# Six small transfers of each segment: issued by SyncE instead of GpSimd

## The chip, the core and the metric

The kernel runs on one core of one Trainium2 chip. The core has TensorE (matrix products, PE in the profile; its weight loads are PEld), VectorE (DVE), ScalarE (ACT), GpSimd (POOL) and SyncE (SP), which computes nothing and here issues most of the transfers. Sixteen DMA engines move the data. The metric is the device time of one execution in microseconds (us); the time of a kernel is the median of several runs.

## The reference

Two independent parts stand side by side in the output, 1024 columns each. Part A is a long convolution over 2048 rows, done with Fourier transforms; it is over before the loop that this document is about. Part B is an attention with a memory that is handed from segment to segment:

```python
for s in range(n_seg):                       # 2048 / 32 = 64 segments
    h = concatenate([mem, x[:, 32*s:32*s+32]], axis=1)      # 8 + 32 rows of 1024
    q, k, v = (einsum('btd,dhe->bhte', h, W) for W in (Wq, Wk, Wv))   # 32 heads of 128
    p = softmax(where(mask, einsum('bhqe,bhke->bhqk', q, k) * scale, -1e9))
    o = einsum('bhqk,bhke->bhqe', p, v)
    o = einsum('bhte,hed->btd', o, Wo)
    mem = o[:, :8]                           # the next segment's memory
    outs.append(o[:, 8:])                    # 32 rows of the result
```

The first 8 rows of a segment's output are needed before the next segment can start, so the 64 segments run one after the other. Every segment uses all four weights, 8 MB each in bf16.

## The kernel before

**The order.** The program is unrolled and its order is the order of the text: each engine works off its own instructions in the order in which they stand. A transfer is an instruction in the stream of the engine that issues it, and that engine goes on as soon as it has handed the transfer over. An instruction that must wait stops what stands behind it on the same engine, transfers too. The profile calls the issuing streams SPq, ACTq and POOLq. Transfers that SyncE issues run in DMA queue q1, those of ScalarE in q10, those of GpSimd in q0.

**The rows.** In the loop (L910) a segment's part on TensorE has 32 rows: 8 of the memory and the first 24 of the segment. The last 8 rows of every segment do not feed the memory. Their q, k and v are made for all segments ahead of the loop and lie in HBM, in `QKBd` and `VBd`. A segment loads its share of them: `qkb` (`load_b`, L793, 128 KB) and `VB` (`load_vb`, L803, 64 KB). Their attention outputs are gathered in `OL` and stored to `OLd` (L860, 64 KB), and their output projection is done for all segments behind the loop (L977 on).

**The weights.** Most of the weights stay in SBUF. Of each segment's weights, 17 pieces of 512 KB (`streamed`, chosen by `STREAM`, L40) come from HBM every time, and two more are parked in PSUM and copied from there (`PARKED`, L41; `unpark`, L716). They go through a ring of `RING = 5` buffers (L39, tile `wring`). `done(key)` (L725) is called behind the last matmul that reads a streamed piece, and `place()` (L708) then issues the load of the piece five places on into the freed buffer, at L713, on SyncE. So a load is issued when TensorE has finished with a piece, and at most five pieces are loaded or being loaded at a time.

**A segment** has four groups `g` of eight heads. `qk_part` makes q and k of a group, `v_part` its v; `scores`, `softmax` and `pv` of a group lie between the products of later groups, and `wo` adds the output projection into the accumulator `Y`. The end of a segment reads: `wo` of group 0, `v_part` of group 3, the load of the next rows (`load_h`, L662, ScalarE), `load_b` for the next segment, `wo` of group 1, `wo` of group 2, `pv` of group 3 with the copy of the last rows' outputs into `OL` (L858, GpSimd) and their store, `wo` of group 3, the copy of `Y` into `Y_sb` (L964, ScalarE), the turn of the memory rows into the next `hT` (`fill_mem`, L965), four stores of `Y_sb` to the result (L970, 12 KB each: 24 rows of 512 bytes), and `load_vb` for the next segment.

**Names for the loads.** Later sections number the 17 weight loads of a segment in the order of their issue. Those around the end are W14 (issued when the second piece of `wo` of group 1 is finished), W15 and W16 (pieces 0 and 3 of `wo` of group 2), W17 (piece 2 of `wo` of group 3), and, in the next segment, W1 (behind `qk_part` piece 5 of group 0), W2 and W3 (behind the first two pieces of `v_part` of group 0). The four stores of `Y_sb` are o1 to o4. With `qkb` the SyncE stream at the end of a segment before the change is: W12, W13, `qkb`, W14, W15, W16, W17, W1, W2, W3. GpSimd's is: copy into `OL`, store of `OL`, o1, o2, o3, o4, load of `VB`.

**Who needs them.** `VB` is read by `pv`, first for group 0 when group 2 is under way. `OL` is written again by the copy of group 0 of the next segment. `Y_sb` shares its one buffer (tag `PT`) with the transposed probabilities of L838, so the softmax of the next segment's group 0 must wait until o1 to o4 have read it. Nobody waits for what the stores wrote to the result.

Of the kernel before, what the change touches and what calls it, by code (L numbers as in the profile page):

```python
# [21 lines left out]
def fused_kernel(ctx: ExitStack, tc, q, k, v, shift_k, ssm_k, ssm_D, outa, x, mem0, Wq, Wk, Wv, Wo, outb, n_seg):  # L22
# [11 lines left out]
    nc = tc.nc  # L34
# [17 lines left out]
    OLd = dram.tile([n_seg, 128, 256], BF, name="OLd")  # L52
    VBd = dram.tile([n_seg, 4, 4, 8, 256], BF, name="VBd")
# [662 lines left out]
    def unpark():  # L716
        while to_copy:
            key, t = to_copy.pop(0)
            nc.scalar.copy(t[:, 0, :], park[key][0][:])  # L719
            nc.vector.tensor_copy(t[:, 1, :], park[key][1][:])  # L720
# [14 lines left out]
    VB = act.tile([128, 256], BF, name="VB")  # L735
    OL = act.tile([128, 32, 8], BF, name="OL")
# [5 lines left out]
    def qk_part(u, kcs):  # L742
        if kcs[0] == 0:
            u.qk = ps_qk.tile([128, 512], F32, tag="qk", name="qkacc")
        for kc in kcs:
            w = pair(("qk", u.g, kc))
            for t in range(2):
                for c2 in range(2):
                    p0 = 32 * (2 * t + c2)
                    nc.tensor.matmul(u.qk[p0:p0 + 32, :], lhsT=hT[:, kc, :], rhs=w[t][:, c2 * 512:(c2 + 1) * 512],  # L750
                                     start=(kc == 0), stop=(kc == 7), tile_position=(0, p0))
            done(("qk", u.g, kc))

    def qk_out(u):
        u.qks = act.tile([128, 512], BF, tag="qks", name="qks")
        nc.scalar.copy(u.qks[:], u.qk[:])  # L756
# [39 lines left out]
    def new_u(g):  # L796
        u = G()
        u.g = g
        u.qkb = qkb[:, g, :]
        return u  # L800

    def load_vb(s):
        nc.gpsimd.dma_start(VB[:], VBd[s].rearrange("c g r x -> (c g r) x"))  # L803

    def scores(u):
        S = ps_ts.tile([128, 4, 40], F32, tag="ts", name="S")
        qb = u.qkb.rearrange("e (h t r) -> e h t r", h=8, t=2)
        for c in range(4):
            nc.tensor.matmul(S[32 * c:32 * c + 32].rearrange("p a k -> p (a k)"), lhsT=ident[:, 32 * c:32 * c + 32],
                             rhs=mask[:].unsqueeze(2).to_broadcast([128, 2, 2, 40]), start=True, stop=False,  # L810
                             tile_position=(0, 32 * c))
        for i in range(2):
            for c in range(4):
                hh = 2 * c + i
                nc.tensor.matmul(S[32 * c:32 * c + 32, i, :], lhsT=u.QT[:, hh, :], rhs=u.KT[:, hh, :],
                                 start=False, stop=False, tile_position=(0, 32 * c))
        for i in range(2):
            for c in range(4):
                hh = 2 * c + i
                nc.tensor.matmul(S[32 * c:32 * c + 8, 2 + i, :], lhsT=qb[:, hh, 0, :], rhs=u.KT[:, hh, :],  # L820
                                 start=False, stop=(i == 1), tile_position=(0, 32 * c))
        mx = act.tile([128, 4], F32, tag="mx", name="mx")
        nc.vector.tensor_reduce(out=mx[:], in_=S[:], op=ALU.max, axis=AX.X)  # L823
        nc.vector.tensor_tensor(out=S[:], in0=S[:], in1=mx[:].unsqueeze(2).to_broadcast([128, 4, 40]), op=ALU.subtract)
        return S

    def softmax(u, S):
        P = act.tile([128, 4, 64], BF, tag="QTP", name="P")
        k0 = 32 + 8 * u.g
        nc.vector.memset(P[:, :, 32:64], 0.0)  # L830
        nc.scalar.activation(P[:, :, 0:32], S[:, :, 0:32], ACT.Exp, scale=scale)
        nc.scalar.activation(P[:, :, k0:k0 + 8], S[:, :, 32:40], ACT.Exp, scale=scale)  # L832
        sm = act.tile([128, 4], F32, tag="sm", name="sm")
        nc.vector.tensor_reduce(out=sm[:], in_=P[:], op=ALU.add, axis=AX.X)  # L834
        nc.vector.reciprocal(sm[:], sm[:])
        nc.vector.tensor_tensor(out=P[:], in0=P[:], in1=sm[:].unsqueeze(2).to_broadcast([128, 4, 64]), op=ALU.mult)
        u.PT = act.tile([128, 4, 2, 32], BF, tag="PT", name="PT")
        nc.vector.transpose(out=u.PT[:].rearrange("p a k q -> p (a k q)"), in_=P[:].rearrange("p a k -> p (a k)"))  # L838

    def pv(u, s, cs, banks="aaaa"):  # L840
        if cs[0] == 0:
            u.OT = act2.tile([128, 8, 40], BF, tag="OT", name="OT")
        PTv = u.PT[:].rearrange("p (a i) k q -> p i k a q", a=2)
        for c in cs:
            pool, tag = {"a": (ps_acc, "acc"), "q": (ps_qk, "qk"), "t": (ps_ts, "ts")}[banks[c]]
            ot = pool.tile([128, 512], F32, tag=tag, name="otacc")
            r = slice(32 * c, 32 * c + 32)
            for i in range(2):
                o = ot[:, 64 * i:64 * i + 64]
                nc.tensor.matmul(o, lhsT=u.v[r, i * 128:(i + 1) * 128], rhs=PTv[r, i, 0], start=True, stop=False,  # L850
                                 tile_position=(32 * c, 0))
                nc.tensor.matmul(o, lhsT=VB[r, i * 128:(i + 1) * 128], rhs=PTv[r, i, 1], start=False, stop=True,  # L852
                                 tile_position=(32 * c, 0))
            ov = ot[:, 0:128].rearrange("e (i q) -> e i q", i=2)
            nc.scalar.copy(u.OT[:, 2 * c:2 * c + 2, :], ov[:, :, 0:40])  # L855
        if cs[-1] == 3:
            to = OL[:] if s + 1 < n_seg else OLs[:, s]
            nc.gpsimd.tensor_copy(to[:, 8 * u.g:8 * u.g + 8, :], u.OT[:, :, 32:40])  # L858
            if u.g == 3 and s + 1 < n_seg:
                nc.gpsimd.dma_start(OLd[s], OL[:].rearrange("e h r -> e (h r)"))  # L860

    def wo(u, Y, hhs=range(8)):
        for hh in hhs:
# [46 lines left out]
    for s in range(n_seg):  # L910
        us = []
        for g in range(4):
            if g == 2 and s + 1 == n_seg:
                spare = [key for key in resident if key[0] != "o" and key[1] < 2 and key not in early]
                for key, at in zip([key for key in streamed if key[0] == "o"], spare):
                    nc.sync.dma_start(res[at][:], Wst[key][:])
                    res[key] = res[at]
            u = new_u(g)
            us.append(u)
            qk_part(u, range(0, 4))  # L920
            unpark()
            if g >= 1:
                S = scores(us[g - 1])
            if g >= 2:
                pv(us[g - 2], s, (0, 1))
            if g >= 1:
                softmax(us[g - 1], S)
            qk_part(u, range(4, 6))
            if g >= 2:
                pv(us[g - 2], s, (2, 3))  # L930
            qk_part(u, range(6, 8))
            qk_out(u)
            if g < 3:
                v_part(u, range(0, 8))
                tr_a(u)
                v_out(u)
            unpark()
            if g == 3 and s + 1 == n_seg:
                for s0, s1 in ((0, 32), (32, s)):
                    nc.sync.dma_start(OLs[:, s0:s1].rearrange("e s h r -> e s (h r)"),  # L940
                                      OLd[s0:s1].rearrange("s e x -> e s x"))
        Y = ps_acc.tile([128, 512], F32, tag="acc", name="yacc")
        wo(us[0], Y)
        tr_a(us[3])
        v_part(us[3], range(0, 8), Y)
        v_out(us[3])
        if s + 1 < n_seg:
            H = load_h(s + 1)
        S = scores(us[3])
        if s + 1 < n_seg:  # L950
            qkb = load_b(s + 1)
        softmax(us[3], S)
        pv(us[2], s, (0, 1), "aqaq")
        wo(us[1], Y, range(0, 4))
        pv(us[2], s, (2, 3), "aqaq")
        wo(us[1], Y, range(4, 8))
        wo(us[2], Y)
        pv(us[3], s, (0, 1, 2, 3), "aqta")
        wo(us[3], Y)
        if s + 1 < n_seg:  # L960
            hT = new_hT()
            h_rows(H, hT, 8)
        Y_sb = act.tile([128, 256], BF, tag="PT", name="Y_sb")
        nc.scalar.copy(Y_sb[:], Y[:, 256:512])  # L964
        if s + 1 < n_seg:  # L965
            fill_mem(hT, Y_sb)
            idle = ps_acc.tile([128, 512], F32, tag="acc", name="idle")
            keep_warm(idle, 2)
        for dq in range(4):
            nc.gpsimd.dma_start(outb[32 * s:32 * s + 24, dq * 256:(dq + 1) * 256], Y_sb[32 * dq + 8:32 * dq + 32, :])  # L970
        if s + 1 < n_seg:
            load_vb(s + 1)

# [87 lines left out]
```

## Time and profile before

| | |
|---|---|
| median of 3 runs | 2194.64 us (2191.91 to 2197.0) |
| the profiled execution's own time | 2189.17 us |
| its span, first to last instruction | 2187.2 us |
| mean granted TensorE clock | 0.956 |
| first and last copy into `Y_sb` (64 segments) | 488.2 and 2125.9 us |
| busy: TensorE, VectorE, ScalarE, GpSimd | 1783.4, 1090.5, 835.3, 405.9 us |
| issue of a weight load on SyncE (L713), median | 320 ns, 1083 of them |
| issue on GpSimd: one store of `Y_sb`, store of `OL`, load of `VB`, median | 508, 547, 563 ns |
| the same from issue to landing, median | 4.8, 5.4, 4.8 us |

The page gives for each engine its busy time and for the 16 DMA engines their mean busy share. From the copies into `Y_sb` the period of the loop follows: the 63rd was at 2094.1 us, so 62 periods took 1605.9 us, 25.9 us each. The rest of the execution lies in part A, ahead of the loop, and in the last rows' projection behind it. A line of the chain of waits says which work or transfer ended last at each point; a line of the waits says who waited, for whom, how long in total, how often, and the longest.

### The profile page before, as it was taken

What the parts mean: (1) busy time and instruction counts of PE and PEld (TensorE: products, weight loads), DVE (VectorE), ACT (ScalarE), POOL (GpSimd) and SP (SyncE); (2) the same over time, 40 slices, a digit from 0 to 9 for tenths busy, and PEclk for the clock granted to TensorE, in tenths of its full rate; (3) what the DMA queues carried; (4) which work ended last, traced back from release to release, by engine and by line L of the source; (5) the groups of instructions that cost most, each with busy time, mean ns of one, the idle gap of its engine ahead of it and who ended that gap; (6) DMA issues with size and microseconds to landing.
All of it is one profiled execution on the core that took longest, in us unless ns stands there. A gap on an engine that the chain in (4) does not pass through costs nothing.

```text
span 2187.2 us, 87959 instructions
## 1 busy us (share of the span) xinstructions
PE 1783.4 (82%) x37808; PEld 1048.2 (48%) x37808; DVE 1090.5 (50%) x3235; ACT 835.3 (38%) x2538; POOL 405.9 (19%) x841
## 2 busy tenths in 40 slices
PE   5777778758888888888888888888888888888889
PEld 2332223325555555554555555545555555555558
DVE  6885652224454555544455455444554545444540
ACT  5445551123333333333444333333333333334320
POOL 4013562101111111111111111111111111111110
PEclk8989899879999999999999999999999999999999
DMA  7798969889999999999999999999999999999990
GB/s 256 266 312 273 314 233 330 267 288 353 347 356 343 373 374 365 368 364 347 370 372 371 370 354 370 362 358 355 368 366 354 363 356 357 371 362 367 359 335 21
DMA packets 275653, 732.15 MB, mean 335 GB/s; under 512 B 65680, under 2 KB 85024, under 8 KB 275262
## 3 DMA queue, kind: packets, MB, share of 16 engines
q1 hardware_dynamic: 214414, 683.05, 84.7%
q0 software_dynamic: 18368, 28.88, 4.2%
q10 hardware_dynamic: 42480, 14.62, 2.7%
q8 instruction: 295, 4.83, 0.9%
q14 instruction: 96, 0.78, 0.1%
HBM read 676.14 MB, written 59.18 MB: 336 GB/s over the span
## 4 chain that ended last, share of the span: by engine, by line
PE 47%; DMA 36%; issue 6%; DVE 4%; ACT 4%; POOL 1%; SPq 0%; ACTq 0%; DVEq 0%; POOLq 0%
DMA wring<-Wstv 17%; PE qkacc L750 13%; PE yacc L867 9%; DMA wring<-Wstqk 7%; PE vacc L765 4%; PE otacc L850 3%; PE yacc L765 3%; PE tp L779 3%; PE pl L984 3%; DMA QKBd<-stq 2%; DMA H<-in_B_x_dram 2%; PE ps_k L177 2%; PE otacc L852 1%; DMA wring<-Wsto 1%; PE ps_q L177 1%
## 5 line engine op out<-in xcount | busy, mean ns | idle before, releaser
L750 PE MATMUL qkacc<-Wqk,hT 128*32 128x512 bf16 x4096 | 351.8, 384 | 3.6 <-issue 3.5
L855 ACT CAST OT<-otacc 128x80 bf16<-128x80 f32 x1024 | 183.8, 235 | 387.4 <-PE otacc L852 381.3
L858 POOL COPY OL<-OT 128x64 bf16<-128x64 bf16 x252 | 63.9, 253 | 1362.3 <-ACT OT L855 1362.3
L765 PEld LDWEIGHTS <-hT 128*32 128x32 bf16 x8192 | 213.8, 97 | 168.7 <-issue 101.9
L750 PEld LDWEIGHTS <-hT 128*32 128x32 bf16 x8192 | 178.3, 96 | 209.9 <-issue 66.7
L867 PE MATMUL yacc<-Wo,OT 128*32 128x256 bf16 x5632 | 253.3, 282 | 26.6 <-issue 21.2
L867 PEld LDWEIGHTS <-OT 128*32 128x32 bf16 x8192 | 213.1, 99 | 90.4 <-issue 58.4
L750 PE MATMUL qkacc<-wring,hT 128*32 128x512 bf16 x2048 | 207.1, 390 | 22.7 <-DMA wring<-Wstqk 20.3
L850 PE MATMUL otacc<-PT,vsb 32*128 32x64 bf16 x2048 | 147.7, 193 | 55.5 <-ACT OT L855 48.7
L765 PE MATMUL vacc<-wring,hT 128*32 128x256 bf16 x2560 | 118.0, 277 | 74.7 <-DMA wring<-Wstv 73.5
L788 DVE COPY QT<-tp 128x256 bf16<-128x256 bf16 x256 | 74.7, 292 | 204.7 <-PE tp L779 198.7
L719 ACT COPY wring<-park 128x1024 bf16<-128x1024 bf16 x128 | 129.9, 1015 | 116.2 <-PE qkacc L750 110.0
L750 PE MATMUL qkacc<-Wearly,hT 128*32 128x512 bf16 x2048 | 167.7, 403 | 7.7 <-DVE hT L893 3.4
L756 ACT CAST qks<-qkacc 128x512 bf16<-128x512 f32 x256 | 150.3, 587 | 47.6 <-PE qkacc L750 44.5
L823 DVE TENSOR_REDUCE mx<-S 128x4 f32<-128x160 f32 x256 | 83.1, 325 | 163.8 <-PE S L820 160.7
L765 PE MATMUL vacc<-Wv,hT 128*32 128x256 bf16 x3584 | 158.4, 274 | 0.7 <-issue 0.7
L834 DVE TENSOR_REDUCE sm<-P 128x4 f32<-128x256 bf16 x256 | 107.5, 420 | 100.6 <-ACT P L832 100.6
L852 PE MATMUL otacc<-PT,VB 32*128 32x64 bf16 x2048 | 144.2, 189 | 11.2 <-issue 10.5
L867 PE MATMUL yacc<-wring,OT 128*32 128x256 bf16 x2520 | 137.1, 281 | 16.4 <-issue 15.4
L885 DVE COPY hT<-x_tp 128x192 bf16<-128x192 bf16 (+1 forms) x64 | 23.0, 359 | 233.8 <-PE x_tp L884 233.8
L970 POOL DMA_DIRECT2D out_dram<-Y_sb x256 | 129.1, 511 | 39.6 <-ACT Y_sb L964 36.3
L850 PEld LDWEIGHTS <-vsb 32*128 32x128 bf16 x2048 | 84.3, 92 | 103.8 <-issue 94.1
(220 smaller groups left out, 2931.9 us busy)
## 6 DMA issues: line engine op xcount, KB each, us to landing
wring<-Wstqk SPq DMA_DIRECT2D x448, 512.0 KB, 6.4
wring<-Wstv SPq DMA_DIRECT2D x320, 512.0 KB, 6.0
wring<-Wsto SPq DMA_DIRECT2D x315, 512.0 KB, 6.0
SK<-s_sb SPq DMA_DIRECT2D x8, 1024.0 KB, 6.5
SU<-s_sb SPq DMA_DIRECT2D x8, 1024.0 KB, 7.8
QKBd<-stq ACTq DMA_DIRECT2D x4, 2048.0 KB, 16.3
Kg<-SK SPq DMA_DIRECT2D x16, 512.0 KB, 6.1
Ug<-SU SPq DMA_DIRECT2D x16, 512.0 KB, 7.2
```

The costliest lines, as they stand in the source:

```text
L719: nc.scalar.copy(t[:, 0, :], park[key][0][:])
L750: nc.tensor.matmul(u.qk[p0:p0 + 32, :], lhsT=hT[:, kc, :], rhs=w[t][:, c2 * 512:(c2 + 1) * 512], start=(kc == 0), stop=(kc == 7), tile_pos ...
L756: nc.scalar.copy(u.qks[:], u.qk[:])
L765: nc.tensor.matmul(u.vacc[32 * c:32 * c + 32, 0:256], lhsT=hT[:, kc, :], rhs=w[kc % 2][:, c * 256:(c + 1) * 256], start=(kc == 0 and Y is ...
L788: nc.vector.tensor_copy(u.QT[:].rearrange("e (c j) r -> e c j r", c=2), tv[:, 0])
L823: nc.vector.tensor_reduce(out=mx[:], in_=S[:], op=ALU.max, axis=AX.X)
L834: nc.vector.tensor_reduce(out=sm[:], in_=P[:], op=ALU.add, axis=AX.X)
L850: nc.tensor.matmul(o, lhsT=u.v[r, i * 128:(i + 1) * 128], rhs=PTv[r, i, 0], start=True, stop=False, tile_position=(32 * c, 0))
L852: nc.tensor.matmul(o, lhsT=VB[r, i * 128:(i + 1) * 128], rhs=PTv[r, i, 1], start=False, stop=True, tile_position=(32 * c, 0))
L855: nc.scalar.copy(u.OT[:, 2 * c:2 * c + 2, :], ov[:, :, 0:40])
L867: nc.tensor.matmul(Y[32 * dq:32 * dq + 32, 256:512], lhsT=u.OT[:, hh, 0:32], rhs=w[hh % 2][:, dq * 256:(dq + 1) * 256], start=(u.g == 0 an ...
L970: nc.gpsimd.dma_start(outb[32 * s:32 * s + 24, dq * 256:(dq + 1) * 256], Y_sb[32 * dq + 8:32 * dq + 32, :])
```

## The change

Three calls change their engine, nothing else:

```diff
     def load_vb(s):
-        nc.gpsimd.dma_start(VB[:], VBd[s].rearrange("c g r x -> (c g r) x"))
+        nc.sync.dma_start(VB[:], VBd[s].rearrange("c g r x -> (c g r) x"))
...
             if u.g == 3 and s + 1 < n_seg:
-                nc.gpsimd.dma_start(OLd[s], OL[:].rearrange("e h r -> e (h r)"))
+                nc.sync.dma_start(OLd[s], OL[:].rearrange("e h r -> e (h r)"))
...
         for dq in range(4):
-            nc.gpsimd.dma_start(outb[32 * s:32 * s + 24, dq * 256:(dq + 1) * 256], Y_sb[32 * dq + 8:32 * dq + 32, :])
+            nc.sync.dma_start(outb[32 * s:32 * s + 24, dq * 256:(dq + 1) * 256], Y_sb[32 * dq + 8:32 * dq + 32, :])
```

In the loop GpSimd keeps its copies into `OL` (L858) and issues no transfer any more. The stream of SyncE at the end of a segment becomes: W12, W13, `qkb`, W14, W15, W16, store of `OL`, W17, o1, o2, o3, o4, load of `VB`, W1, W2, W3. The first `load_vb(0)`, ahead of the loop, moves too. The transfers have the same sources, targets and sizes as before.

## The prediction

> **What bounds the kernel now.** I read the page first (DMA row, chain of waits), then the DMA queues over the loop, then the waits, and then one segment's end in time order: SyncE, GpSimd, chain, and the windows of one microsecond.
>
> ```profile
> DMA  7798969889999999999999999999999999999990
> PE 47%; DMA 36%; issue 6%; DVE 4%; ACT 4%; POOL 1%; SPq 0%; ACTq 0%; DVEq 0%; POOLq 0%
> ```
>
> The DMA engines are busy from the first quarter to the end, and the chain has TensorE and DMA but almost no GpSimd. The queues between 500 and 2100 us, and two waits of TensorE there:
>
> ```profile
> q1 hardware_dynamic: 160270, 559.20, 93.7%
> q0 software_dynamic: 11890, 11.19, 2.3%
> ```
>
> ```profile
> PE vacc L765 <- DMA wring<-Wstv: 60.4, 100, 2.3
> PE qkacc L750 <- DMA wring<-Wstqk: 19.6, 37, 1.4
> ```
>
> With q10, q8 and q14 (0.9, 1.1, 0.1%) the shares add up to 98.1%: the DMA engines' time is the bound, and TensorE waits for weights. What GpSimd issues is 2.3% of it and stays; only its queue changes. So the question is what the move does to the idle 2% and to the time of a packet. One segment's end (SyncE, then GpSimd, then the chain; columns are start, us, what):
>
> ```profile
> 1008.39 0.97 SPq L713 DMA_DIRECT2D wring<-Wstv  x2
> 1010.67 0.32 SPq L713 DMA_DIRECT2D wring<-Wstqk  x1
> 1013.91 0.32 SPq L713 DMA_DIRECT2D wring<-Wstv  x1
> ```
>
> ```profile
> 1010.18 0.24 POOL L858 COPY OL<-OT 128x64 bf16<-128x64 bf16 x1 [1.93 <-ACT OT L855]
> 1010.71 0.55 POOL L860 DMA_DIRECT2D OLd<-OL  x1 [0.29 <-POOL OL L858]
> 1011.55 2.02 POOL L970 DMA_DIRECT2D out_dram<-Y_sb  x4 [0.30 <-ACT Y_sb L964]
> 1013.56 0.56 POOL L803 DMA_DIRECT2D VB<-VBd  x1
> ```
>
> ```profile
> 1012.39 1.51 PE qkacc L750 x24
> 1013.91 5.75 DMA wring<-Wstv
> 1019.70 0.84 PE vacc L765 x24
> ```
>
> W15 and W16 go out from 1008.39 (the second at 1009.04), W17 at 1010.67, and W1 at 1013.91, as soon as TensorE has freed its buffer. W1 is on the chain: its landing at 1019.66 is what TensorE waits for. Where DMA engines idle (the last two columns are DMA share and GB/s):
>
> ```profile
> 1012.00:1013.00 1.00, 0.78 (x14) 0.33 (x16) 0.34 (x2) 0.00 (x0) 1.00 (x3) 1.00 0.90 348
> 1016.00:1017.00 1.00, 1.00 (x40) 0.50 (x32) 0.82 (x3) 0.70 (x1) 0.00 (x0) 1.00 0.80 303
> 1018.00:1019.00 1.00, 0.39 (x5) 0.12 (x6) 0.60 (x3) 0.88 (x3) 0.00 (x0) 1.00 0.84 295
> 1022.00:1023.00 1.00, 1.00 (x32) 0.47 (x32) 0.77 (x3) 0.47 (x3) 0.00 (x0) 1.00 1.02 397
> ```
>
> Early in a segment the share falls to 0.8 to 0.9, later it is full. Over 60 segments, with Y the start of o1, the packets give 0.86 to 0.96 from Y+2.5 to Y+5 and about 1.0 from Y+10 to Y+18. The segment's end is already the thin place of the weights' queue.
>
> **A rule of the transfers that the change meets.** In the issue records each transfer of SyncE or ScalarE takes the next of eight semaphores (100, 102 to 107, 109) in turn, 187 each. Over all pairs whose landing the trace has, none is issued less than 0.02 us after the landing of its semaphore's last user, and many just then. One such wait is visible where no data is shared, a weight load behind ScalarE's store of q and k, eight places earlier:
>
> ```profile
> SPq L678 <- DMA QKBd<-stq: 12.6, 1, 12.6
> ```
>
> So a transfer waits for the landing of the eighth before it. With 19 per segment (17 weights, `qkb`, H) and a ring of five, this never bites in the loop. The change makes it 25, and in the stream W14, W15, W16, store of `OL`, W17, o1 to o4, `VB`, W1, W2, W3 it binds: o4 waits for W14, `VB` for W15, **W1 for W16**, W2 for the store of `OL`, W3 for W17. GpSimd's transfers had eight semaphores of their own (111 to 118).
>
> **The parts.**
>
> *GpSimd loses six issues*, 4 x 0.508 + 0.547 + 0.563 = 3.1 us per segment. It waits 1287.5 us of the loop for `OT`, and nobody waits for it but these transfers: nothing gained.
>
> *SyncE issues six more.* Nearest rows: 0.377 us (`qkb`), 0.421 (final stores, L992). 6 x 0.4 = 2.4 us, beside 18 x 0.32 = 5.8 now, in 25.9: hidden, since o1 to o3 are out by Y+1.2 and W1's buffer is freed at Y+2.0 (median). The store of `OL` stands ahead of W17; the copy ends at 1010.42, so W17 moves from 1010.67 to about 1010.9. Cover: W17 lands 5.7 us after issue, while the quickest load of L713 takes 3.3. Without it, 0.25 x 62 = 16 us.
>
> *o1 to o4 and `VB` in the weights' queue.* They run behind W17 and land near Y+6; from GpSimd, with 4.8 us from issue, they landed at Y+6.3 and Y+6.8. The next writer of their buffer (transpose L838) starts at 1019.46, Y+7.9, and `pv` reads `VB` at Y+10.4. Nothing.
>
> *The packets.* Per segment q0 now has 32 of 4096 bytes at 187 ns, 48 of 1024 at 49 and 111 small ones at 9.1: 9.35 us, 0.58 per DMA engine. On q1 I expect pieces of 512 bytes as on q10 (27.3 ns for H's): 352 x 27.3 + 80 x 9.1 = 10.34 us, 0.65 per engine. That is +0.06 us, or 4 us over the loop. The four stores have 12 packets of two rows each; if the same 12 engines take them every time, those get 24 x 27.3 + 6 x 9.1 = 0.71 us, +0.13, or 8 us. I take 5.
> By the Trainium skill ("DMA: Bandwidth & Descriptors", section "Why a DMA increments its semaphore by 16 and not by 1") a transfer uses the largest number of engines up to 16 that divides its slowest dimension, the lowest-numbered ones on this path. For 24 rows that is always the same 12; by it the term is 8. No row here numbers the engines.
>
> *The wait of W1.* In 60 segments the medians are: W14 lands at Y+0.78, W15 at Y+2.17, W16 at Y+3.67, W17 at Y+5.22; W1 is issued at Y+2.03, W3 at Y+3.61. If W1 must wait for W16 (and `VB` for W15 ahead of it), it goes out 1.53 us later on average; W3 waits for W17, 1.6 later. From issue to first packet takes 1.57 us at the quick end (first landing of a DMA engine less the 1.26 us that 8 packets take there). So the packets of W1 can start at about Y+5.3. An engine is done with W17 between Y+3.2 and Y+5.2, then has 0.65 us of small packets, and then nothing. From each engine's landings I get a mean idle of 0.98 us per segment, against 0.42 worked out in the same way for now: +0.55. Lower bound 0: slow engines set the landing of W1, and they aren't out of work (W17 at Y+5.2, small packets until Y+5.9). Upper bound: all 1.53 us on the path, 62 x 1.53 = 95 us. Some comes back: the fast engines are less far ahead afterwards, and of the 0.05 x 4.5 = 0.2 us that is idle now from Y+5 to Y+9.5 most should fill. I take 0.35, as the DMA time of a segment is the bound: 62 x 0.35 = 22 us.
>
> **Sum:** 0 + 0 + 0 + 5 + 22 = +27 us. Against the profiled execution's own 2189.17 us (span 2187.2 plus 2.0 around it) that is 2216; the median of the runs shown is 5.5 us above it, so I forecast 2194.64 + 27 = **2222 us**, slower by 1.2%. Its own range: 0.1 to 0.55 us of idling and 4 to 8 us of packets, 2205 to 2237; with W17's 16 us, 2253.
>
> **Rivals.**
>
> *The wait is hidden.* For it: W1 lands 5.2 us after issue at the median, and 3.3 is possible; the slack of 1.9 us exceeds the delay of 1.53. Against: the 3.3 are of an empty queue. Then only the packets cost, at times less: 2191 to 2203, likeliest 2198.
> The Trainium skill ("DMA: Bandwidth & Descriptors", section "Issuing engines are not separate DMA queues") speaks for this result: whoever issues, the same 16 DMA engines move the data, and only issue time on the sequencer changes. The shares that add up to 98.1% agree; the eight semaphores are what that section leaves out.
>
> *Faster.* Packets of 4096 bytes on q0 can be long: the loads of `VB` average 205 ns against a usual 159, up to 2008. In the segment shown W1's last engine comes 3.3 us after W17's, where the median is 1.8. The longest q0 packet of a segment has a median of 0.39 us; if it always lies on the engine that lands last, and short pieces remove it, 62 x (0.39 - 0.16) = 14 us go: 2181. It decides where the delay of W1 stays within its slack. Against it: q1 has 30 packets over 0.5 us per segment of its own.
>
> *The whole delay shows.* Were W1's landing governed by its issue, all 95 us would come: 2290. The chain has W1 on it; against it, the 5.75 us there are mostly queueing.
>
> *The semaphores aren't shared in this way:* that is the first rival again.
>
> **How the numbers follow.** Chances: forecast 0.60, hidden 0.18, faster 0.15, whole delay 0.07. What can be told from no change here is 0.2%, about 4.4 us: 2190.2 to 2199. Slower: 0.60 + 0.07 + the hidden case's upper part, 0.05 = 0.72; same: 0.12 of the hidden case; faster: 0.15 and 0.01 of it. The range from 2182 to 2252 leaves out the whole delay, half of the faster case and a little of the forecast's top.
>
> **What would show it.** q0 gone from the loop, and q1 with some 430 more packets per segment, at about 27 ns. W1 issued just behind W16's landing, near Y+3.7 instead of Y+2.0, with SyncE waiting at L803 or L970 for weights. The DMA share between Y+3 and Y+5.5 lower than 0.86, the loop's mean share down from 98.1% to about 97%, the period up from 25.9 to 26.3 us. GpSimd's waits mean nothing. Wrong: if W1 goes out at Y+2 as before, the semaphore rule is not as read; if it goes out late and the period stays, the slow engines alone set the pace; if L838 or `pv` wait for o4 or `VB`, I have missed a wait.

## The result, and the profile after

| | before | changed |
|---|---|---|
| median | 2193.27 us (4 runs, 2183.92 to 2197.0) | 2218.55 us (4 runs, 2213.92 to 2224.78) |
| ratio, 95% interval | | 1.0123 (1.009 to 1.0155) |
| ratio in a second set, on another chip | 2190.49 us | 2217.22 us, 1.0107 (1.0076 to 1.0138) |
| profiled execution's own time, span | 2189.17, 2187.2 us | 2214.47, 2212.6 us |
| first and last copy into `Y_sb` | 488.2, 2125.9 us | 482.8, 2150.7 us |

The changed kernel is slower by 25 us, 1.2%. In the two profiled executions the loop itself, from the first copy into `Y_sb` to the last, is 30.2 us longer (1637.7 and 1667.9). The part ahead of it is 5.4 us shorter in the changed execution; in the other profiled executions of this study the first copy lies anywhere from 482.8 to 489.0.

The chain of waits of the changed kernel, by engine and by line:

```profile
PE 44%; DMA 42%; issue 5%; DVE 4%; ACT 4%; POOL 1%; SPq 1%; ACTq 0%; DVEq 0%; POOLq 0%
DMA wring<-Wstv 24%; PE qkacc L750 11%; PE yacc L867 9%; DMA wring<-Wstqk 7%; PE vacc L765 3%; PE yacc L765 3%; DMA wring<-Wsto 3%; PE otacc L850 3%; PE pl L984 3%; PE tp L779 2%; DMA QKBd<-stq 2%; PE ps_k L177 2%; PE ps_q L177 1%; PE ps_v L174 1%; PE otacc L852 1%
```

The second of these lines, for the kernel before:

```profile
DMA wring<-Wstv 17%; PE qkacc L750 13%; PE yacc L867 9%; DMA wring<-Wstqk 7%; PE vacc L765 4%; PE otacc L850 3%; PE yacc L765 3%; PE tp L779 3%; PE pl L984 3%; DMA QKBd<-stq 2%; DMA H<-in_B_x_dram 2%; PE ps_k L177 2%; PE otacc L852 1%; DMA wring<-Wsto 1%; PE ps_q L177 1%
```

The queues of the changed kernel between 500 and 2100 us (packets, MB, share of the 16 DMA engines):

```profile
q1 hardware_dynamic: 183630, 559.73, 93.5%
q8 instruction: 262, 4.29, 1.1%
q10 hardware_dynamic: 8784, 4.00, 0.9%
q14 instruction: 78, 0.64, 0.1%
```

DMA has gone from 36% to 42% of the chain, nearly all of it in loads of v weights (17% to 24%); W1 and W4, among the first loads of a segment, are such loads. GpSimd's queue q0 is gone. Yet the shares now add up to 95.6% where they were 98.1%: the DMA engines, which bound the loop, have less to do per unit of time. The waits in the same stretch (engine, line, what it waited for, us in total, times, longest):

```profile
PE vacc L765 <- DMA wring<-Wstv: 76.4, 125, 2.5
PE qkacc L750 <- DMA wring<-Wstqk: 39.2, 55, 1.9
```

```profile
SPq L860 <- POOL OL L858: 72.3, 61, 3.1
SPq L803 <- DMA wring<-Wstv: 29.2, 34, 2.3
SPq L970 <- DMA wring<-Wstqk: 6.4, 12, 1.0
```

TensorE waits longer for weights (60.4 and 19.6 us before). SyncE waits at L803 and L970 for the landing of weights: the load of `VB` and the stores of `Y_sb` share no data with a weight. One segment's end on SyncE, whose copy into `Y_sb` starts at 1009.80:

```profile
1007.30 0.97 SPq L713 DMA_DIRECT2D wring<-Wstv  x2
1009.42 0.39 SPq L860 DMA_DIRECT2D OLd<-OL  x1
1009.90 0.38 SPq L713 DMA_DIRECT2D wring<-Wstqk  x1
1010.38 1.64 SPq L970 DMA_DIRECT2D out_dram<-Y_sb  x4
1012.88 0.35 SPq L803 DMA_DIRECT2D VB<-VBd  x1
1014.20 0.35 SPq L713 DMA_DIRECT2D wring<-Wstv  x1
1014.65 1.36 SPq L713 DMA_DIRECT2D wring<-Wstqk  x2
```

After o4 the stream stands until 1012.88, and after `VB` until 1014.20, when W1 goes out 4.4 us behind the copy. The trace shows which semaphore each instruction sets and waits for: W16 set 104, and the wait of W1 that ended at 1014.2 was for 104, which W1 then uses itself. In the same way o4 waited for 102 (W14) and `VB` for 103 (W15). What that leaves for the DMA engines (last two columns: share and GB/s):

```profile
1013.00:1014.00 1.00, 1.00 (x36) 0.74 (x25) 0.24 (x2) 0.93 (x2) 0.00 (x0) 1.00 0.97 374
1014.00:1015.00 1.00, 0.95 (x24) 0.46 (x19) 0.05 (x1) 0.49 (x3) 0.00 (x0) 1.00 0.59 191
1015.00:1016.00 1.00, 1.00 (x29) 0.46 (x25) 1.00 (x3) 0.92 (x2) 0.00 (x0) 1.00 0.81 209
1017.00:1018.00 1.00, 0.65 (x28) 0.45 (x23) 0.59 (x3) 0.84 (x3) 0.00 (x0) 1.00 0.45 143
```

From 1014 on the engines run out of weights; in the window that starts there small packets take half of the busy time, and 191 GB/s are moved. Over 60 segments the packets fill 0.68 of the engines' time from 3 to 5.5 us behind the start of o1, where they filled 0.93 before. Over the same 60 segments, in us behind the start of the copy into `Y_sb`:

| mean | W16 lands | W17 lands | W1 issued | W1 lands | W3 issued | W3 lands |
|---|---|---|---|---|---|---|
| before | 4.34 | 5.87 | 2.93 | 7.93 | 4.38 | 10.98 |
| changed | 4.13 | 5.74 | 4.28 | 8.19 | 5.90 | 11.85 |

W1 goes out just behind the landing of W16, W3 behind that of W17. What reaches TensorE is a fifth of W1's delay (0.26 of 1.35 us), but more than half of W3's (0.87 of 1.52).

### The profile page after: what moved, and what is told of

Read it like the earlier page. It is cut to its first block, busy times and chain, and to the rows that moved or that the text cites. A ratio compares the mean times of both kernels' runs of the same rounds, so it can differ in the third digit from the quotient of the medians.

```text
span 2212.6 us, 87953 instructions
## 1 busy us (share of the span) xinstructions
PE 1781.1 (80%) x37808; PEld 1050.7 (47%) x37808; DVE 1089.4 (49%) x3235; ACT 836.2 (38%) x2538; POOL 205.7 (9%) x458
## 4 chain that ended last, share of the span: by engine, by line
PE 44%; DMA 42%; issue 5%; DVE 4%; ACT 4%; POOL 1%; SPq 1%; ACTq 0%; DVEq 0%; POOLq 0%
DMA wring<-Wstv 24%; PE qkacc L750 11%; PE yacc L867 9%; DMA wring<-Wstqk 7%; PE vacc L765 3%; PE yacc L765 3%; DMA wring<-Wsto 3%; PE otacc L850 3%; PE pl L984 3%; PE tp L779 2%; DMA QKBd<-stq 2%; PE ps_k L177 2%; PE ps_q L177 1%; PE ps_v L174 1%; PE otacc L852 1%
## 5 line engine op out<-in xcount | busy, mean ns | idle before, releaser
L858 POOL COPY OL<-OT 128x64 bf16<-128x64 bf16 x252 | 62.5, 248 | 1647.2 <-ACT OT L855 1647.2
L765 PE MATMUL vacc<-wring,hT 128*32 128x256 bf16 x2560 | 116.8, 275 | 96.5 <-DMA wring<-Wstv 94.9
L719 ACT COPY wring<-park 128x1024 bf16<-128x1024 bf16 x128 | 129.9, 1015 | 116.3 <-PE qkacc L750 99.3
L750 PE MATMUL qkacc<-Wearly,hT 128*32 128x512 bf16 x2048 | 163.0, 395 | 7.7 <-DVE hT L893 3.8
L774 ACT CAST vsb<-vacc 128x256 bf16<-128x256 f32 x192 | 71.5, 373 | 162.6 <-PE vacc L765 162.3
```

The source lines that it names most:

```text
L765: nc.tensor.matmul(u.vacc[32 * c:32 * c + 32, 0:256], lhsT=hT[:, kc, :], rhs=w[kc % 2][:, c * 256:(c + 1) * 256], start=(kc == 0 and Y is ...
L774: nc.scalar.copy(u.v[:], u.vacc[:, 0:256])
```

## The experiments

Three theories stood against each other. **The count:** transfers of SyncE and ScalarE take eight semaphores in turn, so each waits for the landing of the eighth before it, and the six more push W1 to W3 up against W16 and W17. **The queue:** small packets among the weights, some of them on 12 of the 16 engines only, cost DMA time. **The order:** SyncE's stream stands at the waits for `OL` and `Y_sb`, and weight loads stand behind it. Each kernel was timed beside the kernel before on the same chip.

### One half of the change, then the other

e1_stores moves o1 to o4 only:

```diff
-            nc.gpsimd.dma_start(outb[32 * s:32 * s + 24, dq * 256:(dq + 1) * 256], Y_sb[32 * dq + 8:32 * dq + 32, :])
+            nc.sync.dma_start(outb[32 * s:32 * s + 24, dq * 256:(dq + 1) * 256], Y_sb[32 * dq + 8:32 * dq + 32, :])
```

> The four stores of Y_sb are issued by SyncE, the store of OL and the load of VB stay on GpSimd. Theory of the count (the eighth transfer back must have landed): 23 transfers per segment; the eighth before W1 is W14, before W2 W15, before W3 W16. In the kernel before these land before or just as W1, W2 and W3 are issued (W16 at 4.34 us after the copy into Y_sb, W3 at 4.38), so the time is that of the kernel before, 0 to +6 us, and W1 goes out near 2.9 us after the copy. Theory of the queue (small packets among the weights, twelve engines carrying the stores): these stores are the part that is uneven, so a third to two thirds of the 25 us, +8 to +16. Theory of the order (SyncE's stream stands at the wait for Y_sb): up to half, +12.

Measured: 2186.89 against 2192.15 us, ratio 0.9978 (0.9954 to 1.0003).

e2_ol_vb moves the other two only:

```diff
-        nc.gpsimd.dma_start(VB[:], VBd[s].rearrange("c g r x -> (c g r) x"))
+        nc.sync.dma_start(VB[:], VBd[s].rearrange("c g r x -> (c g r) x"))
...
-                nc.gpsimd.dma_start(OLd[s], OL[:].rearrange("e h r -> e (h r)"))
+                nc.sync.dma_start(OLd[s], OL[:].rearrange("e h r -> e (h r)"))
```

> The store of OL and the load of VB are issued by SyncE, the four stores of Y_sb stay on GpSimd. Theory of the count: 21 transfers per segment, the eighth before W1 was issued ahead of W14 and has long landed: 0 to +4 us. Theory of the queue: two thirds of the 432 small packets are here, +8 to +16 us. Theory of the order: the store of OL, which waits for GpSimd's copy, is the only moved transfer with a weight load (W17) right behind it; if that wait cost the time, most of it is here, +10 to +25 us.

Measured: 2183.75 against 2192.15 us, ratio 0.998 (0.9951 to 1.0009).

Each half alone costs nothing; if anything it gives 0.2%, which the intervals don't settle. Together they cost 1.2%. A price per transfer, per packet or per wait in the stream would add up; a limit that is reached only by both does not. W1 goes out at 2.95 us in e1_stores and 2.92 in e2_ol_vb, as before (2.93). The theory of the order falls by a line of e2_ol_vb's waits on SyncE:

```profile
SPq L860 <- POOL OL L858: 69.9, 61, 2.3
```

SyncE stands there for 69.9 us in 61 segments, as long as in the changed kernel (72.3), and the time does not change: what stands behind, W17, is in no hurry.

### The turn of the semaphores alone

e3_tiny6 leaves all six transfers on GpSimd and adds six stores of 64 bytes to SyncE's stream, at the same places. They write a scratch tensor that nobody reads.

```diff
+    def tiny(s, i):
+        nc.sync.dma_start(TNd[s, i:i + 1, :], ident[0:1, 0:32])
...
                 nc.gpsimd.dma_start(OLd[s], OL[:].rearrange("e h r -> e (h r)"))
+                tiny(s, 0)
...
         if s + 1 < n_seg:
+            for i in range(5):
+                tiny(s, 1 + i)
             load_vb(s + 1)
```

> The kernel before with six stores of 64 bytes (one partition of ident into a scratch tensor) added to SyncE's stream in each of 63 segments, at the six places of the changed kernel: one ahead of W17, five ahead of W1. Nothing is moved, and they wait for no data. Theory of the count: W1 must wait for W16, W2 for the first small store, W3 for W17, as in the changed kernel, so +15 to +28 us, with W1 issued about 4.3 us after the copy into Y_sb instead of 2.9. Theory of the queue: six packets of 64 bytes per segment are nothing, 0 to +3 us. Theory of the order: 0 us.

Measured: 2227.17 against 2192.15 us, ratio 1.0173 (1.0136 to 1.021), +35 us and so above the expected range. W1 goes out at 4.40 us, W3 at 6.00. SyncE's waits in this kernel (L740 is the tiny store):

```profile
SPq L714 <- DMA wring<-Wstv: 168.3, 206, 3.2
SPq L740 <- DMA wring<-Wstv: 57.6, 55, 2.3
SPq L740 <- DMA wring<-Wstqk: 30.0, 44, 2.3
```

A tiny store reads a constant and writes scratch, and yet it waits for weights to land. Six transfers with next to nothing in them reproduce the place of W1 and the whole loss, and some 10 us more.

### How many it takes

The same tiny stores, all between W17 and W1, four, five and eight per segment:

```diff
+            for i in range(N):        # 4, 5 or 8
+                tiny(s, 1 + i)
```

> The kernel before with four stores of 64 bytes in SyncE's stream between W17 and W1, none ahead of W17. Theory of the count: the eighth before W1 is W14, which lands 1.4 us after the copy into Y_sb; W1 goes out at 2.9 as before. 0 to +5 us. If the cost were one of a small store each (issue on SyncE, a landing in HBM), four would cost two thirds of what six did (+38 us): +25.

> As e6_tiny4 with five. Theory of the count: W1 waits for W15 (lands at 2.8 us, no delay), W2 for W16 (4.3 instead of 3.8), W3 for W17 (5.9 instead of 4.4). +5 to +20 us: the part of the cost that W3's wait makes without W1's. At a cost for each store: +32.

> As e6_tiny4 with eight. Theory of the count: the eighth small store waits for W17, W1 for the first small store behind it in the stream, so W1 goes out near 6 us after the copy into Y_sb, 3 us late, and starts its packets near 7.5. By the idle time worked out as in the prediction 1.4 us more per segment: +65 to +115 us, with a DMA share below 0.5 around 6 to 7 us after the copy. At a cost for each store: +50.

| tiny stores | W1 waits for | W1 issued | period | idle per segment | ratio (95% interval) |
|---|---|---|---|---|---|
| none (before) | | 2.93 | 25.9 | 0.5 us | 1 |
| 4 | W14 | 2.98 | 26.1 | 0.7 us | 0.9988 (0.996 to 1.0016) |
| 5 | W15 | 3.27 | 26.3 | 1.0 us | 1.0088 (1.0053 to 1.0123) |
| 8 | first tiny store | 6.37 | 27.9 | 2.9 us | 1.0593 (1.0549 to 1.0636) |

W1's issue is the mean in us behind the copy into `Y_sb`; the period is that of the profiled execution; idle is the period times what the queues' shares leave of 1. (The profiled execution with four took 2199.7 us, 15 more than that kernel's median, so its period and idle time are on the high side.) Four cost nothing, eight cost 126 us: the cost does not go by the number of transfers but by whose landing W1 has to wait for. With five, W1 is hardly late (0.34 us), but W2, which now waits for W16, goes out at 4.51 instead of 3.84, and W3, which waits for W17, at 5.97 instead of 4.38. That costs 16 us with little wait of W1, so the loads behind it matter too. With eight my range (up to +115) was too low. One segment's end there:

```profile
1019.40 0.32 SPq L714 DMA_DIRECT2D wring<-Wstqk  x1
1019.77 8.01 SPq L740 DMA_DIRECT2D TNd<-ident  x8
1027.88 0.34 SPq L714 DMA_DIRECT2D wring<-Wstv  x1
```

```profile
1023.00:1024.00 1.00, 0.84 (x24) 0.65 (x25) 0.00 (x0) 0.48 (x1) 0.00 (x0) 1.00 0.93 371
1024.00:1025.00 1.00, 0.01 (x2) 0.00 (x1) 0.00 (x0) 0.00 (x0) 0.48 (x1) 1.00 0.62 206
1025.00:1026.00 1.00, 1.00 (x20) 0.57 (x23) 0.24 (x2) 0.56 (x2) 0.60 (x2) 1.00 0.17 43
1027.00:1028.00 1.00, 0.41 (x27) 0.31 (x30) 0.00 (x0) 0.00 (x0) 0.00 (x0) 1.00 0.02 6
```

SyncE needs 8 us for the eight stores, since the last four of them wait for W14, W15, W16 and W17 to land, and W1 goes out only at 1027.88. The DMA share falls from 0.93 to 0.02 meanwhile: what was a thin place before is an empty queue here.

### Another issuer, another queue

e4_act has all six on ScalarE:

```diff
-        nc.gpsimd.dma_start(VB[:], VBd[s].rearrange("c g r x -> (c g r) x"))
+        nc.scalar.dma_start(VB[:], VBd[s].rearrange("c g r x -> (c g r) x"))
...
-                nc.gpsimd.dma_start(OLd[s], OL[:].rearrange("e h r -> e (h r)"))
+                nc.scalar.dma_start(OLd[s], OL[:].rearrange("e h r -> e (h r)"))
...
-            nc.gpsimd.dma_start(outb[32 * s:32 * s + 24, dq * 256:(dq + 1) * 256], Y_sb[32 * dq + 8:32 * dq + 32, :])
+            nc.scalar.dma_start(outb[32 * s:32 * s + 24, dq * 256:(dq + 1) * 256], Y_sb[32 * dq + 8:32 * dq + 32, :])
```

> All six are issued by ScalarE (queue q10, not the weights' queue; SyncE's stream is that of the kernel before). The eight semaphores are shared by SyncE and ScalarE. Theory of the count: W1 still has W16 as the eighth before it, W3 W17: +15 to +30 us, W1 near 4.3 us after the copy into Y_sb. Theory of the queue: the weights have their queue for themselves, 0 to +6 us. Theory of the order: SyncE waits for nothing new; ScalarE stands a little, 0 to +8 us.

Measured: 2239.18 against 2192.15 us, ratio 1.0222 (1.0184 to 1.0259), more than expected. Its waits, SyncE first, then ScalarE:

```profile
SPq L713 <- DMA OLd<-OL: 158.2, 40, 6.1
```

```profile
ACT wring L719 <- DMA wring<-Wstv: 44.4, 17, 4.1
```

SyncE's own stream is that of the kernel before, and still a weight load, W1, waits for ScalarE's store of `OL`: the turn is shared between the two. W1 goes out at 4.59 us. What it waits for is not what I had expected. In the turn the store of `OL` stands ahead of W16 here, although it is issued behind it, so W1 has the semaphore of that store, W2 that of W16 and W3 that of o1; in 55 of 62 segments W1 goes out less than 0.2 us behind the landing of the store of `OL`. So with two issuing engines the turn has to be read from the semaphores in the trace, not from the order of issue. The weights' queue q1 holds none of the six here, which speaks against the queue as the cause. On top of it ScalarE itself now stands: its load of `VB` goes out less than 0.2 us behind the landing of W15 in 47 of 63 segments, and the copy of a parked weight (L719) stands behind that load. This fits the larger loss, and was not tried by itself.

### The same transfers in another order

e5_spread is the changed kernel with `VB`'s load behind W3 and the store of `OL` behind W4 of the next segment:

```diff
             if kc % 2 == 1:
                 done(("v", u.g, kc // 2))
+            if u.g == 0 and kc == 3 and s > 0:
+                load_vb(s)
...
-            if u.g == 3 and s + 1 < n_seg:
-                nc.sync.dma_start(OLd[s], OL[:].rearrange("e h r -> e (h r)"))
...
             qk_part(u, range(0, 4))
+            if g == 1 and s > 0:
+                nc.sync.dma_start(OLd[s - 1], OL[:].rearrange("e h r -> e (h r)"))
...
-        if s + 1 < n_seg:
-            load_vb(s + 1)
```

> All six are issued by SyncE as in the changed kernel, but two stand later in its stream: the load of VB behind W3, the store of OL (of the segment before) behind W4. The same transfers in the same queue, 25 per segment; only the order differs: W14, W15, W16, W17, o1 to o4, W1, W2, W3, VB, W4, OL. Theory of the count: the eighth before W1 is W14, before W2 W15, before W3 W16, before W4 o1, all landed by then or nearly, so the 25 us vanish: -8 to +4 us against the kernel before. What can spoil it: VB now lands behind W3, about 11 us after the copy into Y_sb, just as pv first reads it, worth up to 0.5 us per segment or +30 us, and then TensorE waits for VB. Theory of the queue (as many small packets among the weights, on the same engines): +15 to +28 us as in the changed kernel.

Measured: 2204.69 against 2190.68 us, ratio 1.0072 (1.0046 to 1.0099). W1 is back at 2.95 us, but the time only partly. TensorE's waits name what was feared (L854 is the line of `pv` that reads `VB`):

```profile
PEld L854 <- DMA VB<-VBd: 43.1, 54, 2.3
PE otacc L854 <- DMA VB<-VBd: 37.0, 52, 2.2
```

And the turn holds up the load of `VB` itself (L805), which I had not counted: behind W3 it has W17 as the eighth before it.

```profile
SPq L805 <- DMA wring<-Wstqk: 42.2, 51, 1.9
```

It goes out at 5.75 us, just behind the landing of W17 (5.66), and lands at 11.3; `pv` reads it at 11.4, where it did at 10.8 before. So this run tells little by itself on the queue. e9_five takes the load of `VB` back to GpSimd and keeps the rest of e5_spread:

> As e5_spread, but the load of VB is back on GpSimd, so that nobody waits for it: five of the six are issued by SyncE, o1 to o4 behind W17 and the store of OL behind W4, 24 transfers per segment. Theory of the count: W1 to W4 wait for nothing new, so none of the 25 us: -14 to +4 us against the kernel before; the low end if the small packets are cheaper in the weights' queue than in GpSimd's, as the times of e1_stores, e2_ol_vb and e3_tiny6 beside the changed kernel suggest. Theory of the queue: 288 of the 432 packets are there and the uneven ones among them, +12 to +20 us.

Measured: 2192.22 against 2190.49 us, ratio 0.9992 (0.9968 to 1.0017). Five of the six transfers, with o1 to o4 and their uneven share among them, run in the weights' queue and cost nothing that can be told, as long as W1, W2 and W3 have no later landing to wait for than those of W14, W15 and W16. That holds W3 up a little: it goes out at 4.81 us instead of 4.38. The theory of the queue falls with it.

> The changed kernel itself, beside e9_five on one chip, for a narrower interval: +19 to +32 us against the kernel before. e3_tiny6 has the same waits and none of the moves and took 1.7% more; if the moves by themselves cost nothing, this too comes out at 1.7%, if they give time back it stays near 1.2%.

Measured in the same set: 2217.22 us, ratio 1.0107 (1.0076 to 1.0138), against 1.0173 (1.0136 to 1.021) for e3_tiny6. The moves seem to give some 0.5% back, as e1_stores and e2_ol_vb hint; e9_five, with a ratio of 0.9992, doesn't bear it out. This stays open. None of the kernels is clearly faster than the kernel before.

## Why the prediction was right

*What bounds the kernel.* The DMA engines' time: right, as the shares and the periods go together (with none, five and eight tiny stores 0.5, 1.0 and 2.9 us idle per segment, and periods of 25.9, 26.3 and 27.9).

*The eight semaphores, and W1 behind W16, W2 behind the store of `OL`, W3 behind W17.* Right, seen in each instruction's semaphore and shown by e3_tiny6 and the series of four, five and eight. W1 was put at Y+3.7, which is 4.3 us behind the copy into `Y_sb`; it is at 4.28.

*GpSimd's six issues, SyncE's six, W17's delay, `VB` and `Y_sb` landing in time: nothing.* Right. GpSimd's busy time fell from 405.9 to 205.7 us with no gain; W17 is 0.18 us later (forecast 0.25), and e2_ol_vb shows that this is free; no wait for `VB` or o4 stands among the changed kernel's longest.

*The term of the wait, 22 us.* Its mechanism was right and its size too small. I had 0.55 us of idling per segment and took 0.2 off for what comes back. Idle went from 0.49 us (1.9% of 25.9) to 1.16 (4.4% of 26.4; I had put it at about 3% of 26.3), +0.67, or 41 us over 62 periods. I had priced W1's wait and put no price on W3's, which I had named; the run with five tiny stores shows that the waits of W2 and W3, with only 0.34 us of W1's, are worth 16 us.

*The term of the packets, +5 us.* The small packets behaved as put down: 28.1 ns for 512 bytes (forecast 27.3), 432 more packets per segment on q1 (forecast some 430). But the busy time of a segment fell, from 25.4 to 25.2 us, since the weights' own packets became a little shorter: 172.4 ns on average instead of 174.3, with 20 over 0.5 us per segment instead of 30. That is -0.2 us, or -12 us, where I had +5. The two errors point in opposite directions: together some 30 us in the loop, as measured, where I had 27. In the second set's profile (173.3 ns, 24 long ones) the fall is smaller. Part of the agreement is luck.

By the Trainium skill ("DMA: Bandwidth & Descriptors", section "Why a DMA increments its semaphore by 16 and not by 1") a store of 24 rows runs on 12 engines, and the sequencer itself writes the missing four counts at once. The trace agrees: each of o1 to o4 makes 13 updates of its semaphore, the first a median of 0.53 us after its issue, then 12 as data lands. That the uneven load costs time, e9_five doesn't show.

*The rivals.* Hidden: no, though W1's landing is only 0.26 us later. The 3.3 us of the quickest load were put down to an empty queue; that load is a W1, issued when W17 still had 0.75 us to its landing. In the changed kernel W1 takes 3.9 us from issue to landing on average, where it took 5.0, so most of its own delay is indeed hidden, and the loss is idle time of the DMA engines. Faster: not in this form. The whole delay: no; 1.35 us x 62 = 84 us would have come, and 25 did. With eight tiny stores 3.4 us x 62 = 213 would have come, and 126 did.

## What to carry to other kernels

Before a small transfer is put into a stream that feeds the bound of a kernel, count the transfers in it: if semaphores are handed out in turn, the n-th must wait for the landing of an earlier one, whatever the two carry and whichever of the engines that share the turn issued it. Look for waits between transfers that share no data, and check which landing the important load would come to wait for; one transfer fewer, or the same ones elsewhere, can make the whole difference. When two halves of a change are free and the whole isn't, look for a count.

## What had not been expected

The weights' packets of 4096 bytes are shorter in some of the kernels whose DMA engines idle more: 174.3 ns on average before (98.1% busy), 172.4 in the changed kernel (95.6%), 171.7 with eight tiny stores (89.6%), and packets over 0.5 us fall from 30 to 20 and 19 per segment. It is no rule: e3_tiny6 has 174.2 ns and 31 long packets at 96.1%, e4_act 173.5 ns and 29 at 94.9%. What shortens the packets was not tried.
